# Squares by VectorE's clock, and key weights in a second ring, in a four-layer attention kernel

## The chip, the core and the metric

The kernel runs on one core of a Trainium2 chip. The metric is the device time of one execution in microseconds (us). Instructions run on TensorE (PE in the profile, its weight loads PEld), VectorE (DVE), ScalarE (ACT) and GpSimd (POOL); SyncE's queue (SP) issues all the transfers. Each engine takes its instructions in the order in which they stand in its queue.

## The reference

Four attention layers with a residual each; 2048 tokens, 512 features, 32 heads of 16. Layers 0 and 2 use weights A and a sliding window of 256, layers 1 and 3 weights B and the whole sequence.

```python
def _B_ref(x, wqkv, wo):                  # full; _A_ref adds the window's mask
    B, S, D = x.shape                     # 1, 2048, 512
    H = 32; Dh = D // H
    qkv = (x @ wqkv).reshape(B, S, 3, H, Dh).transpose(2, 0, 3, 1, 4)
    q, k, v = qkv[0], qkv[1], qkv[2]
    p = softmax(einsum("bhqd,bhkd->bhqk", q, k) * Dh ** -0.5)
    o = einsum("bhqk,bhkd->bhqd", p, v)
    return o.transpose(0, 2, 1, 3).reshape(B, S, D) @ wo

x = A_x
x = x + _A_ref(layernorm(x), A_wqkv, A_wo)
x = x + _B_ref(layernorm(x), B_wqkv, B_wo)
x = x + _A_ref(layernorm(x), A_wqkv, A_wo)
x = x + _B_ref(layernorm(x), B_wqkv, B_wo)
```

## The kernel before

**Scores.** A full layer works in quads of four heads (qd, 8 of them; two quads are a head tile) and in four chunks c of 512 queries. For a quad and a chunk, each of 16 key tiles gives two scores s (two heads each, 128 keys x 1024): TensorE multiplies kt by qt (L756), ScalarE takes the exponential of the 128 x 1024 score (e<-s, L764), and TensorE multiplies e by the values into acc (L809). A quad so has 32 scores and a full layer 1024. Layer 1 runs chunk by chunk, layer 3 head tile by head tile (t, four of 256 scores). After a quad, `epilogue` joins the two halves of acc on VectorE (sa, ot), divides (op), and every second quad stores oh, the input of the output projection.

**The softmax's shift.** No maximum of a score is taken. Instead half the sum of the largest squared key and the squared query is subtracted: rows of -0.515 times the squares stand beside q and k, so the score's matmul subtracts them. For that every projection of keys or queries leaves squares sq (GpSimd, L528; ScalarE in the tails, L526). A job `rest` in the list `pend` later sums them over the 16 dims on TensorE (`squares`: a matmul with hsum, L550, in the tails L553), and VectorE makes of the sums the maximum km of the keys (L569) or the queries' row m (L584, L585), which a transfer writes beside the queries in DRAM (qs<-m, L597). `key_shift` makes the keys' row mk out of km (L608, L613) and writes it to kf. The scores' operands qt and kt are read from qs and kf, so these must be there first.

**Side work.** Projections of other chunks, head tiles or layers (L400: 48 matmuls of 512 columns, two halves of the rows each, for 128 features; 96 of 256 columns for values), layer norm and the output projection run between the scores. `Work` is one of them: K1, K3 keys of a head tile for layers 1 and 3; Q3 queries; VV values; OO, O3 output projection; T transposes. `Side` deals them out: after every second score of a quad `step` calls `share`, which first may run the due jobs of `pend` and then one or several matmuls' worth of the projection under way. What it decides by are clocks of a model: `clock[0]` for TensorE, `vt_[0]` for VectorE, `PH["free"]` for the bank. `PH["busy"]` says that a projection is half done. `finish` forces what is left at the end of a stage (a chunk in layer 3). The result is an order written out for TensorE, and in full layers for VectorE too; the other engines' orders come from the tile scheduler.

**The bank.** In a full layer all this side work has one pair of PSUM banks, b (`PH["halves"]`): a projection, or a set of squares, must have been read by VectorE before the next one may begin.

**Weights.** `weights` takes a buffer from one of two rings: ring 0, tag w, two buffers; ring 1, tag vw, three buffers, in the windowed layers used for value tiles. `may_open` says when a load may be issued. Work marked `act` runs in the tail behind a windowed layer, where neither kind of attention runs: `tails[0]` ends with the last chunk's K1(0) and K1(1), `tails[2]` with K3(3, 0), and then the next layer's first values come (`lasts`).

Of the kernel before, what the change touches and what calls it, by code (L numbers as in the profile page):

```python
# [190 lines left out]
def fast_path(ctx, tc, flag, a_x, a_wqkv, a_wo, b_wqkv, b_wo, out):  # L191
# [293 lines left out]
    def project(l, s, c, act, ht=None):  # L485
# [3 lines left out]
        w = weights(ty, s, n, *((0, D, 0) if ht is None else (ht * P, (ht + 1) * P, l == 3 and not act)))  # L489
# [70 lines left out]
    def keys(l, c, act, ht=None, then=None):  # L560
        sqs = yield from project(l, 1, c, act, ht)

        def rest():
            ph = squares(f"k{l}_{c}_{ht}", sqs)
            if l not in KM:
                KM[l] = vp.tile([P, NQ], F32, name=f"km{l}", tag="km", bufs=2)
            r = quarters(ht)
            with tc.high_priority(HEAD_START):
                nc.vector.tensor_reduce(KM[l][r, c:c + 1], ph[r], axis=AX.XY if PH["full"] else AX.X, op=ALU.max)  # L569
                if then is not None:  # L570
                    then(l, ht)
        pend.append((clock[0] + (4.6 if PH["full"] else 3.6), rest))

    def queries(l, c, act, ht=None):
        sqs = yield from project(l, 0, c, act, ht)
# [22 lines left out]
        pend.append((clock[0] + (4.6 if PH["full"] else 3.6), rest))  # L598
# [111 lines left out]
    def epilogue(l, c, qd, a):  # L710
# [14 lines left out]
        def scaled():  # L725
            den = ot[:, :, DH]
            nc.vector.tensor_tensor(lmin, lmin, den, ALU.min)
            nc.vector.tensor_add(lsum, lsum, den)
            r = vp.tile([P, QC // 32], F32, name=f"r{n}", tag="r")
            nc.vector.tensor_scalar_max(r, den, L_MIN)  # L730
            nc.vector.reciprocal(r, r)
            if u == 0:
                OT[t] = vp.tile([P, QC // 32, 2, DH], F32, name=f"op{n}", tag="op", bufs=1)
            nc.vector.tensor_tensor(OT[t][:, :, u, :], ot[:, :, :DH], r[:, :, None].broadcast_to([P, QC // 32, DH]), ALU.mult)

# [114 lines left out]
    class Work:  # L850
# [25 lines left out]
        def may_open(self):  # L876
# [4 lines left out]
                    (len(wused[self.ring]) < RINGS[self.ring] or wused[self.ring][-RINGS[self.ring]].done) and (PH["full"] or not self.ring)  # L881
# [31 lines left out]
    class Side:  # L913
# [65 lines left out]
        def share(self):  # L979
# [3 lines left out]
            if pend and not PH["busy"] and clock[0] >= max(PH["free"], pend[0][0]):  # L983
                settle(False)
                PH["free"] = clock[0] + 2.0
                self.lag += 0.1
# [9 lines left out]
        def finish(self, keep=False):  # L996

            stays = lambda w: (w.name is None and keep) if w.name is None else w.name[0] == "P"
            while any(not stays(w) for w in self.q):
                self.one(True)  # L1000
# [87 lines left out]
    def K3(c, ht, act=False):  # L1088
        return Work(later(keys, 3, c, act, ht, key_shift if c == NQ - 1 and ht == 0 else None), PK / 4, ("K3", c, ht), [("T", 3, c)], True, ring=not act)

    def Q3(c, ht, act=False, after=()):
        return Work(later(queries, 3, c, act, ht), PK / 4, ("Q3", c, ht), [("T", 3, c), *after], True, ring=not act)

    def K1(ht, act=False):
        return Work(later(keys, 1, NQ - 1, act, ht, key_shift), PK / 4, ("K1", ht), [("T", 1, NQ - 1), ("P", 1, 1)], True)

    def shift3(ht):
        def gen():
            settle()
            key_shift(3, ht)  # L1100
            yield -1e-6
        return Work(gen(), 0.0, ("S3", ht), [("K3", c, ht) for c in range(NQ)])
# [115 lines left out]
    def side3(t, c):  # L1218
        a = [last_lower(3)] if (t, c) == (0, 0) else []
        a += [Q3(c + 1, t)] if c < 3 else []  # L1220
        if t < 3:
            a.append(K3(c, t + 1))
            if c == 3:
                a += [shift3(t + 1), Q3(0, t + 1)]
        if t < 2 and (t or c > 1):
            a.append(upper(3, 2 * t + c // 2, range(2 * (c % 2), 2 * (c % 2) + 2)))
        if (t, c) != (0, 0):
# [7 lines left out]
             2: [VV(3, 0, True, (0,)), OO(2, 3, True), VV(3, 1, True, (0,), late(3)), VV(3, 2, True, (0,), late(3)), VV(3, 0, True, (1,), late(3)), T(3, 3), K3(3, 0, True)]}  # L1235
# [54 lines left out]
```

## Time and profile before

| | us |
|---|---|
| timed runs | 2723.14, 2723.62, 2728.02; median 2723.62 |
| profiled execution, its own time | 2721.88 |
| its span | 2720.2 |
| busy: TensorE / ScalarE / VectorE / GpSimd | 2487.6 / 2363.1 / 1110.8 / 526.7 |
| layer 1, first to last exponential | 474.23 to 1425.45 |
| layer 3, first to last exponential | 1746.01 to 2700.19 |
| tail behind layer 0, behind layer 2 | 48.3, 45.1 |

The times below are from the profiled execution; its span is shorter than its time by 1.7 us. The granted TensorE clock over the whole execution was 0.988 of full speed. In a row of a timeline stand the start, the busy time, engine, line and operation, out<-in, the number of instructions, and in brackets the idle time ahead of it and what ended it.

### The profile page before, as it was taken

How to read it: one execution, taken by the hardware profiler on the slowest of the kernel's cores; microseconds unless marked ns; L12 is line 12 of the kernel's file. 1: busy time of each engine (PE TensorE's matmuls, PEld its weight loads, DVE VectorE, ACT ScalarE, POOL GpSimd, SP SyncE). 2: the span in 40 equal slices, each digit the busy share in tenths (PEclk: the TensorE clock that was granted, in tenths of full speed). 3: DMA queues.
4: the chain of work that ended last, by engine and by line, in shares of the span. 5: the costliest groups of instructions: out<-in, count | busy, mean ns of one | idle time of the engine just before them, and what ended most of it. 6: DMA issues, size and time to landing. Idle time of an engine off the chain costs nothing.

```text
span 2720.2 us, 113346 instructions
## 1 busy us (share of the span) xinstructions
PE 2487.6 (91%) x51023; PEld 1095.7 (40%) x51023; DVE 1110.8 (41%) x2342; ACT 2363.1 (87%) x2671; POOL 526.7 (19%) x1080
## 2 busy tenths in 40 slices
PE   7888999999998999999998999899999999988997
PEld 3233444444443444444443333544444444433332
DVE  5574554223434334334326666323333323333333
ACT  4575664999999999999995777499999999999996
POOL 1455551001100100100105778000000000000000
PEclk9999999999999999999999999999999999999999
DMA  8888865222324225333426565623233333334332
GB/s 283 233 253 248 241 193 162 82 90 86 108 91 126 92 90 138 94 100 102 110 71 192 160 194 148 167 72 117 81 107 100 96 96 105 109 106 123 122 118 98
DMA packets 341159, 360.80 MB, mean 133 GB/s; under 512 B 117800, under 2 KB 256568, under 8 KB 334392
## 3 DMA queue, kind: packets, MB, share of 16 engines
q1 hardware_dynamic: 340664, 353.46, 43.7%
q8 instruction: 401, 6.57, 1.0%
q14 instruction: 94, 0.77, 0.1%
HBM read 240.65 MB, written 96.99 MB: 124 GB/s over the span
## 4 chain that ended last, share of the span: by engine, by line
ACT 55%; PE 23%; issue 11%; DVE 7%; DMA 3%; POOL 1%; SPq 0%; ACTq 0%; DVEq 0%; POOLq 0%
ACT e L764 55%; PE b L403 9%; PE acc L842 4%; PE s L760 2%; PE acc L809 2%; PE s L756 2%; PE bs L403 1%; PE b L400 1%; DVE xh L455 1%; DVE xh L449 1%; DMA kt<-kw 1%; DVE xn L449 0%; DVE ot L723 0%; DMA wr<-in_A_wo_dram 0%; DMA wv<-wd 0%
## 5 line engine op out<-in xcount | busy, mean ns | idle before, releaser
L764 ACT ACTIVATE e<-s 128x1024 f32<-128x1024 f32 (+2 forms) x2432 | 2240.7, 1056 | 149.9 <-PE s L760 101.0
L809 PE MATMUL acc<-e,vt 64*17 64x512 f32 x16384 | 1085.6, 590 | 1.0 <-issue 1.0
L756 PE MATMUL s<-qt,kt 64*32 64x512 f16 x16384 | 850.8, 381 | 121.4 <-ACT e L764 99.8
L756 PEld LDWEIGHTS <-kt 64*32 64x32 f16 x16384 | 407.0, 89 | 931.3 <-issue 852.0
L809 PEld LDWEIGHTS acc<-e,vt 64*17 64x17 f32 x16384 | 281.0, 92 | 61.8 <-issue 3.8
L835 POOL TENSOR_SCALAR_AFFINE_SELECT e<-e 128x256 f32<-128x256 f32 x512 | 224.9, 445 | 189.7 <-ACT e L764 188.5
L832 POOL TENSOR_SCALAR_AFFINE_SELECT e<-e 128x256 f32<-128x256 f32 x448 | 199.2, 450 | 94.4 <-ACT e L764 91.9
L842 PE MATMUL acc<-e,vt 128*17 128x384 f32 (+2 forms) x2816 | 201.8, 394 | 6.4 <-POOL e L832 6.2
L741 POOL TENSOR_TENSOR oh<-o,oh 128x512 f16<-128x512 f32 x31 | 36.1, 1163 | 702.0 <-DVE oh L740 676.0
L403 PE MATMUL b<-xc,w 128*128 128x512 f16 x660 | 161.7, 392 | 9.8 <-DVE km L569 5.5
L706 DVE SCALAR_TENSOR_TENSOR x<-b,x 128x512 f32<-128x512 f32 x122 | 83.9, 688 | 193.1 <-PE b L400 189.8
L760 PE MATMUL s<-qt,kt 64*128 64x384 f16 (+2 forms) x1408 | 121.3, 279 | 43.7 <-ACT e L764 20.4
L422 DVE TENSOR_SCALAR sa<-acc 128x512 f32<-128x512 f32 x64 | 44.2, 691 | 281.4 <-PE acc L809 281.4
L528 POOL TENSOR_TENSOR sq_h<-sp_h 128x512 bf16<-128x512 f16 x29 | 42.9, 1479 | 546.4 <-DVE sp_h L522 537.6
L528 POOL TENSOR_TENSOR sq<-sp 128x512 bf16<-128x512 f16 x32 | 46.2, 1443 | 519.7 <-DVE sp L522 475.2
L400 PE MATMUL b<-xc,w 64*32 64x512 f16 x3072 | 126.5, 376 | 2.7 <-DVE j L423 1.5
L400 PE MATMUL b<-xc,w_h 64*32 64x512 f16 x2784 | 111.0, 376 | 3.9 <-DVE km L569 3.9
L400 PE MATMUL b<-wo,oh 64*32 64x512 f16 x2592 | 109.1, 376 | 5.4 <-DVE x L706 3.0
L403 PEld LDWEIGHTS <-w 128*128 128x128 f16 x720 | 67.0, 100 | 116.3 <-issue 46.4
L422 DVE TENSOR_SCALAR vt<-b 128x256 f32<-128x256 f32 (+1 forms) x36 | 18.4, 512 | 232.9 <-PE b L400 232.9
L760 PEld LDWEIGHTS <-kt 64*128 64x128 f16 x1408 | 52.0, 95 | 140.9 <-issue 114.8
L422 DVE TENSOR_SCALAR j_h<-b 128x512 f32<-128x512 f32 x29 | 20.0, 689 | 206.6 <-PE b L400 206.6
(134 smaller groups left out, 1905.9 us busy)
## 6 DMA issues: line engine op xcount, KB each, us to landing
kt<-kf SPq DMA_DIRECT2D x128, 512.0 KB
qt<-qs SPq DMA_DIRECT2D x128, 256.0 KB
xd<-x SPq DMA_DIRECT2D x96, 256.0 KB
x<-xd SPq DMA_DIRECT2D x96, 256.0 KB
w<-wd SPq DMA_DIRECT2D x21, 1024.0 KB
kt<-kw SPq DMA_DIRECT2D x64, 256.0 KB
qs<-sp SPq DMA_DIRECT2D x48, 256.0 KB
wo<-wd SPq DMA_DIRECT2D x12, 1024.0 KB
```

Source lines behind the costliest of these rows:

```text
L400: nc.tensor.matmul(ps[g:g + 32, r], a[k, g:g + 32], b[k], start=(i == 0), stop=(i == len(pairs) - 1), skip_group_check=True)
L403: nc.tensor.matmul(ps, a, b, start=(i == 0), stop=(i == len(pairs) - 1))
L422: nc.vector.tensor_scalar(dst, ps[0], scale, None, op0=ALU.mult)
L528: nc.gpsimd.tensor_tensor(sq, sp[:, 0], sp[:, 0], ALU.mult)
L706: nc.vector.scalar_tensor_tensor(xs[i], p, 1 / WS, xs[i], op0=ALU.mult, op1=ALU.add)
L756: nc.tensor.matmul(ps[g:g + 32, h], kt[R * h:R * h + R, pr, kc + g:kc + g + 32], qt[R * h:R * h + R, pr], start=True, stop=True, skip_grou ...
L760: nc.tensor.matmul(ps[:, h, s0:s0 + wd_], kt[R * h:R * h + R, pr, kc:kc + P], qt[R * h:R * h + R, pr, qc:qc + wd_], start=True, stop=True)
L764: nc.scalar.activation(e[:, :, w0:w1], ps[:, :, w0:w1], AF.Exp, scale=SCALE)
L809: nc.tensor.matmul(acc[r][32 * h:32 * h + DH + 1, :], V[l, qd // 4, j // 8][k, j % 8, 4 * (qd % 4) + h, :], es_[h // 2][k, h % 2, :], star ...
L832: nc.gpsimd.affine_select(v, v, pattern=[[0, 2], [-1, P]], compare_op=ALU.is_gt, fill=0.0, base=0, channel_multiplier=1)
L835: nc.gpsimd.affine_select(v, v, pattern=[[0, 2], [1, P]], compare_op=ALU.is_ge, fill=0.0, base=0, channel_multiplier=-1)
L842: nc.tensor.matmul(a[32 * h:32 * h + DH + 1, q * P:(q + nb) * P], V[l, (4 * c + j) // 4][:, j % 4, 4 * qd + h, :], es_[h // 2][:, h % 2, s ...
```

## The change

It has six parts. (1) In the tails the key weights of K1(0), K1(1) and K3(3, 0) come from ring 1 instead of ring 0; `may_open` allows ring 1 wherever no windowed attention runs. (2) Outside attention a job of `pend` falls due 1.2 us after its projection by the model instead of 3.6. (3) `share` runs such a job only when VectorE's modelled clock, less 0.2, has passed as well. (4) `finish` goes on while a projection is half done and a job is pending. (5) The work `shift3`, which ran all pending jobs and then formed a head tile's shift ahead of Q3(0, t+1), is gone: each head tile's shift is formed in the job of its last keys, K3(3, ht). (6) In `epilogue`, lmin and lsum are updated behind the division.

```diff
@@ -482,11 +482,11 @@
             yield "wait", XNR[l, c] + 2.3 * i
             transposed(l, c, i, xh)
 
-    def project(l, s, c, act, ht=None):
+    def project(l, s, c, act, ht=None, ring=0):
 
 
         ty, n = l % 2, f"{l}_{s}_{c}" + ("" if ht is None else f"_h{ht}")
-        w = weights(ty, s, n, *((0, D, 0) if ht is None else (ht * P, (ht + 1) * P, l == 3 and not act)))
+        w = weights(ty, s, n, *((0, D, 0) if ht is None else (ht * P, (ht + 1) * P, ring)))
         yield wait(8)
         xc = XC[l, c]
         if s == 0:
@@ -557,8 +557,8 @@
 
         return slice(0, P) if ht is None else slice(32 * ht, 32 * ht + 32)
 
-    def keys(l, c, act, ht=None, then=None):
-        sqs = yield from project(l, 1, c, act, ht)
+    def keys(l, c, act, ht=None, then=None, ring=0):
+        sqs = yield from project(l, 1, c, act, ht, ring)
 
         def rest():
             ph = squares(f"k{l}_{c}_{ht}", sqs)
@@ -569,10 +569,10 @@
                 nc.vector.tensor_reduce(KM[l][r, c:c + 1], ph[r], axis=AX.XY if PH["full"] else AX.X, op=ALU.max)
                 if then is not None:
                     then(l, ht)
-        pend.append((clock[0] + (4.6 if PH["full"] else 3.6), rest))
-
-    def queries(l, c, act, ht=None):
-        sqs = yield from project(l, 0, c, act, ht)
+        pend.append((clock[0] + (4.6 if PH["full"] else 3.6 if PH["win"] else 1.2), rest))
+
+    def queries(l, c, act, ht=None, ring=0):
+        sqs = yield from project(l, 0, c, act, ht, ring)
 
         def rest():
             ph = squares(f"q{l}_{c}_{ht}", sqs)
@@ -595,7 +595,7 @@
                     nc.vector.tensor_scalar(m, ph, kx, -0.515, op0=ALU.add, op1=ALU.mult)
             for t in sqs:
                 nc.sync.dma_start(rows(qs[l % 2, c])[8 * t:8 * t + 8, 3, :], m[32 * t:32 * t + 8, :])
-        pend.append((clock[0] + (4.6 if PH["full"] else 3.6), rest))
+        pend.append((clock[0] + (4.6 if PH["full"] else 3.6 if PH["win"] else 1.2), rest))
 
     def settle(all_=True):
         while pend and (all_ or pend[0][0] <= clock[0]):
@@ -724,14 +724,14 @@
 
         def scaled():
             den = ot[:, :, DH]
-            nc.vector.tensor_tensor(lmin, lmin, den, ALU.min)
-            nc.vector.tensor_add(lsum, lsum, den)
             r = vp.tile([P, QC // 32], F32, name=f"r{n}", tag="r")
             nc.vector.tensor_scalar_max(r, den, L_MIN)
             nc.vector.reciprocal(r, r)
             if u == 0:
                 OT[t] = vp.tile([P, QC // 32, 2, DH], F32, name=f"op{n}", tag="op", bufs=1)
             nc.vector.tensor_tensor(OT[t][:, :, u, :], ot[:, :, :DH], r[:, :, None].broadcast_to([P, QC // 32, DH]), ALU.mult)
+            nc.vector.tensor_tensor(lmin, lmin, den, ALU.min)
+            nc.vector.tensor_add(lsum, lsum, den)
 
         def parts():
             o = vp.tile([P, QC], F32, name=f"o{n}", tag="o", bufs=1)
@@ -878,7 +878,7 @@
             return (all(d in DONE for d in self.deps if d[0] == "P") and
                     all(d[1:] in ONR or d[1] % 2 == 0 and d[2] for d in self.deps if d[0] == "O") and
                     all(("N",) + d[1:] in DONE for d in self.deps if d[0] == "T") and
-                    (len(wused[self.ring]) < RINGS[self.ring] or wused[self.ring][-RINGS[self.ring]].done) and (PH["full"] or not self.ring)
+                    (len(wused[self.ring]) < RINGS[self.ring] or wused[self.ring][-RINGS[self.ring]].done) and not (PH["win"] and self.ring)
                     and not (self.adds and any(x.adds and not x.done for x in wused[0])))
 
         done = begun = open = going = False
@@ -980,7 +980,7 @@
 
             self.budget = min(self.budget + max((self.cost - self.spent) / max(self.steps - 3 - self.k, 1), self.least), 0.75)
             self.lag = max(self.lag - 0.42, -0.3)
-            if pend and not PH["busy"] and clock[0] >= max(PH["free"], pend[0][0]):
+            if pend and not PH["busy"] and clock[0] >= max(PH["free"], pend[0][0], vt_[0] - 0.2):
                 settle(False)
                 PH["free"] = clock[0] + 2.0
                 self.lag += 0.1
@@ -996,7 +996,7 @@
         def finish(self, keep=False):
 
             stays = lambda w: (w.name is None and keep) if w.name is None else w.name[0] == "P"
-            while any(not stays(w) for w in self.q):
+            while any(not stays(w) for w in self.q) or PH["busy"] and pend:
                 self.one(True)
             carried.extend(self.q)
 
@@ -1085,21 +1085,15 @@
         k = [("K", l, i) for i in (c - 1, c) if i >= 0] if l % 2 == 0 else list(after)
         return Work(later(queries, l, c, act), PK, ("Q", l, c), [("T", l, c), ("P", l % 2, 0)] + k, True)
 
-    def K3(c, ht, act=False):
-        return Work(later(keys, 3, c, act, ht, key_shift if c == NQ - 1 and ht == 0 else None), PK / 4, ("K3", c, ht), [("T", 3, c)], True, ring=not act)
+    def K3(c, ht, act=False, ring=None):
+        ring = not act if ring is None else ring
+        return Work(later(keys, 3, c, act, ht, key_shift if c == NQ - 1 else None, ring), PK / 4, ("K3", c, ht), [("T", 3, c)], True, ring=ring)
 
     def Q3(c, ht, act=False, after=()):
-        return Work(later(queries, 3, c, act, ht), PK / 4, ("Q3", c, ht), [("T", 3, c), *after], True, ring=not act)
+        return Work(later(queries, 3, c, act, ht, not act), PK / 4, ("Q3", c, ht), [("T", 3, c), *after], True, ring=not act)
 
     def K1(ht, act=False):
-        return Work(later(keys, 1, NQ - 1, act, ht, key_shift), PK / 4, ("K1", ht), [("T", 1, NQ - 1), ("P", 1, 1)], True)
-
-    def shift3(ht):
-        def gen():
-            settle()
-            key_shift(3, ht)
-            yield -1e-6
-        return Work(gen(), 0.0, ("S3", ht), [("K3", c, ht) for c in range(NQ)])
+        return Work(later(keys, 1, NQ - 1, act, ht, key_shift, act), PK / 4, ("K1", ht), [("T", 1, NQ - 1), ("P", 1, 1)], True, ring=act)
 
     def O3(c, ht):
         return Work(wo_part(c, ht), PO / 4, None, [("O", 3, c, ht)], True)
@@ -1221,7 +1215,7 @@
         if t < 3:
             a.append(K3(c, t + 1))
             if c == 3:
-                a += [shift3(t + 1), Q3(0, t + 1)]
+                a.append(Q3(0, t + 1))
         if t < 2 and (t or c > 1):
             a.append(upper(3, 2 * t + c // 2, range(2 * (c % 2), 2 * (c % 2) + 2)))
         if (t, c) != (0, 0):
@@ -1232,7 +1226,7 @@
              [side3(t, c) for t in range(NHT) for c in range(NQ)]]
     late = lambda l: [("N", l, 3)]
     tails = {0: [VV(1, 2, True, (0,)), OO(0, 3, True), VV(1, 1, True, (0, 1), late(1)), VV(1, 0, True, (1,), late(1)), T(1, 3), K1(0, True), K1(1, True)],
-             2: [VV(3, 0, True, (0,)), OO(2, 3, True), VV(3, 1, True, (0,), late(3)), VV(3, 2, True, (0,), late(3)), VV(3, 0, True, (1,), late(3)), T(3, 3), K3(3, 0, True)]}
+             2: [VV(3, 0, True, (0,)), OO(2, 3, True), VV(3, 1, True, (0,), late(3)), VV(3, 2, True, (0,), late(3)), VV(3, 0, True, (1,), late(3)), T(3, 3), K3(3, 0, True, True)]}
     lasts = {l: [VV(l + 1, 3, True, (0,), (), range(2))] for l in (0, 2)}
     for l in range(4):
         if l % 2 == 0:
```

How this moves instructions. First SyncE's queue in tail 0, as a difference (before with -, after with +). w_1_3_h are the weights of K1(0) and K1(1), wv_3_0 those of the values that follow, x the residual's rows, sp_1_3_h the projected keys.

```order
 L477 DMA_TRANSPOSE xc_3_5388<-xh_3_3_5403 128x8x128
 L469 DMA x_3_12044<-xd 128x512
-L371 DMA w_1_3_h_5472<-wd_1_110 128x8x128
-L371 DMA w_1_3_h_5530<-wd_1_110 128x8x128
-L371 DMA wv_3_0_0_5552<-wd_2_111 128x8x256
-L533 DMA kf<-sp_1_3_h_0_5545 128x2x512
-L534 DMA kf<-sp_1_3_h_0_5545 128x512
+L371 DMA wv_3_0_0_5476<-wd_2_111 128x8x256
```

The two key weights leave this place (the first now stands in the last chunk of layer 0, the second ahead of the load of wv_1_0_0 in the early tail), and the value weights follow the last x load. In tail 2 the load of K3(3, 0)'s weights moves in the same way into layer 2, to the place of Q3(1, 0)'s, which goes into the tail.

Next TensorE in layer 3, the squares of the last keys of head tile 2 (sq3_1_3_h2; s3_3_2 and s3_3_3 are scores of the two quads of head tile 1, last chunk). Before:

```order
L756 MATMUL s3_3_2_13_1_44094<-qt3_3_2_43491,kt3_3_2_1_43495 32x512
L550 LDWEIGHTS hsum_86
L550 MATMUL b3_33394<-sq3_1_3_h2_2_44071,hsum_86 32x512
L550 LDWEIGHTS hsum_86
L550 MATMUL b3_33394<-sq3_1_3_h2_2_44071,hsum_86 32x512
L400 LDWEIGHTS w3_0_0_h2_43559
L400 MATMUL b3_33394<-xc3_0_30736,w3_0_0_h2_43559 32x512
```

After:

```order
L756 MATMUL s3_3_3_6_1_44536<-qt3_3_3_43540,kt3_3_3_0_43542 32x512
L550 LDWEIGHTS hsum_86
L550 MATMUL b3_33396<-sq3_1_3_h2_2_44185,hsum_86 32x512
L550 LDWEIGHTS hsum_86
L550 MATMUL b3_33396<-sq3_1_3_h2_2_44185,hsum_86 32x512
L756 LDWEIGHTS kt3_3_3_0_43542
L756 MATMUL s3_3_3_7_0_44555<-qt3_3_3_43540,kt3_3_3_0_43542 32x512
```

The squares stand 18 scores later, and scores follow them where a projection (L400) on the same bank followed before; the next user of b comes four or five scores later.

Last TensorE in layer 3, the squares of Q3(1, 1) (sq3_0_1_h1) and K3(0, 2) (sq3_1_0_h2). Before, the first of them:

```order
L756 MATMUL s3_0_3_4_1_39999<-qt3_0_3_39098,kt3_0_3_0_39100 32x512
L550 LDWEIGHTS hsum_86
L550 MATMUL b3_33394<-sq3_0_1_h1_1_39655,hsum_86 32x512
L550 LDWEIGHTS hsum_86
L550 MATMUL b3_33394<-sq3_0_1_h1_1_39655,hsum_86 32x512
L756 LDWEIGHTS kt3_0_3_0_39100
L756 MATMUL s3_0_3_5_0_40023<-qt3_0_3_39098,kt3_0_3_0_39100 32x512
```

After, both:

```order
L756 MATMUL s3_0_3_8_1_40226<-qt3_0_3_39098,kt3_0_3_1_39102 32x512
L550 LDWEIGHTS hsum_86
L550 MATMUL b3_33396<-sq3_0_1_h1_1_39655,hsum_86 32x512
L550 LDWEIGHTS hsum_86
L550 MATMUL b3_33396<-sq3_0_1_h1_1_39655,hsum_86 32x512
L550 LDWEIGHTS hsum_86
L550 MATMUL b3_33396<-sq3_1_0_h2_2_40013,hsum_86 32x512
L550 LDWEIGHTS hsum_86
L550 MATMUL b3_33396<-sq3_1_0_h2_2_40013,hsum_86 32x512
L756 LDWEIGHTS kt3_0_3_1_39102
L756 MATMUL s3_0_3_9_0_40246<-qt3_0_3_39098,kt3_0_3_1_39102 32x512
```

Before, the keys' squares stood 12 scores behind the queries'; now one set follows the other on b, eight scores later than the first stood. Such pairs stand at five places of layer 3, and at none before. At the program's end the last output projection but one (O3(2, 3), L400) is dealt out over earlier scores, so that none of it is left behind the last score; before, 32 of its matmuls stood there.

## The prediction

> **What bounds the kernel now.** I read the page first, then one table of stages, then the chain of waits and the timelines at the stage ends and at the holes in ScalarE's row. Each row of the table is a stretch, its length, and the busy time of each engine in it:
>
> ```profile
> core 0: us, PE busy (x) PEld busy (x) DVE busy (x) ACT busy (x) POOL busy (x), PEclk, DMA share, GB/s
> 426.00:474.20 48.20, 44.29 (x278) 24.71 (x270) 20.89 (x51) 11.73 (x26) 1.95 (x6) 0.96 0.56 162
> 474.20:1425.50 951.30, 898.88 (x22916) 407.84 (x22924) 337.39 (x666) 944.84 (x1024) 67.73 (x52) 1.00 0.33 98
> 1701.00:1746.00 45.00, 39.37 (x308) 27.18 (x307) 19.19 (x47) 10.59 (x24) 1.12 (x3) 1.00 0.70 192
> 1746.00:2700.20 954.20, 871.78 (x21750) 387.19 (x21742) 309.03 (x580) 943.99 (x1024) 57.23 (x42) 1.00 0.34 104
> 2700.20:2720.20 20.00, 7.18 (x70) 2.27 (x69) 9.84 (x25) 0.00 (x0) 0.00 (x0) 0.79 0.32 110
> ```
>
> The two full layers (rows 2 and 4) hold 70% of the span, and ScalarE's exponentials fill them: 1024 in 951.3 us is 0.93 us a score, and ScalarE is idle for only 6.5 and 10.2 us. So there a change can win no more than those holes, and loses whenever TensorE comes late with a score. In the tails (rows 1 and 3) and at the end TensorE and the chain behind it set the time. The change touches holes, tails and end, so the forecast is a sum of small terms.
>
> **Tail 0: key weights in the other ring.** Before, the first key projection waits for its weights, and the value projection after it for the next ones. Timeline of TensorE, then two pieces of the chain:
>
> ```profile
> 456.63 1.47 PE L403 MATMUL bs<-wv,xc 128*128 128x256 f16 x12
> 457.94 1.47 PE L403 MATMUL b<-wv,xc 128*128 128x256 f16 x12
> 460.49 2.76 PE L403 MATMUL bs<-xc,w_h 128*128 128x512 f16 x12 [1.08 <-DMA w_h<-wd]
> 463.09 2.75 PE L403 MATMUL b<-xc,w_h 128*128 128x512 f16 x12
> 468.41 1.81 PE L403 MATMUL b<-wv,xc 128*128 128x256 f16 x12 [2.24 <-DMA wv<-wd]
> 470.14 0.61 PE L553 MATMUL bs<-sq_h,hsum 128*32 128x512 bf16 x1
> 456.91 3.53 DMA w_h<-wd
> 463.28 5.08 DMA wv<-wd
> ```
>
> Starts of equal groups lie 1.31 us apart (456.63, 457.94) for 256 columns and 2.60 (460.49, 463.09) for 512. With both key weights in place the keys run from 457.94 + 1.31 = 459.25 to 464.45. The value weights now follow the last x load at 456.91, in the place where w_h stood; 3.53 to 5.08 us later is 460.4 to 462.0, before 464.45. One value group of 1.31 and the first squares bring the second squares (L553, which the first scores wait for) to 466.0 instead of 470.14: **-4.1** (-3.4 to -4.4; everything behind L553 moves along). Cover: the new weights must land during layer 0's end and early tail. If they only swap places with the value weights in a busy stretch, one wait of 1.08 to 2.24 comes back. The Trainium skill, "DMA: Bandwidth & Descriptors", Issuing engines are not separate DMA queues, says that all transfers share the same 16 engines and interleave; that speaks against a gain from reordering them alone. By that rule the tails' two terms would be 0 where the engines are full, and the sum -0.4. This tail's row shows a DMA share of 0.56, so that case is a rival below, priced from rows.
>
> A rule on the clock: the Trainium skill, "TensorE: Matmul & The Clock Gate", What's actually happening, has the clock fall to half after an idle window of about 3.4 us. The trace differs, since here
>
> ```profile
> 468.40:471.00 2.60, 2.59 (x15) 1.53 (x16) 0.21 (x1) 0.38 (x1) 0.00 (x0) 0.70 0.86 267
> 477.00:480.00 3.00, 3.00 (x80) 1.25 (x65) 0.00 (x0) 2.02 (x3) 0.00 (x0) 0.56 0.92 284
> ```
>
> ```profile
> 480.05 4.69 ACT L764 ACTIVATE e<-s 128x1024 f32<-128x1024 f32 x5 [0.99 <-PE s L756]
> ```
>
> 0.70 was granted after TensorE had idled 2.24 us, and 0.56 with 0.99 us of hole behind it. A tail with less idle time may start layer 1 without that hole, or only move it: I take 0, bounds -1 to +0.6.
>
> **Tail 2.** The same wait, for one key group:
>
> ```profile
> 1734.66 1.47 PE L403 MATMUL bs<-wv,xc 128*128 128x256 f16 x12
> 1737.46 2.76 PE L403 MATMUL b<-xc,w_h 128*128 128x512 f16 x12 [1.33 <-DMA w_h<-wd]
> ```
>
> Its weights load during layer 2 now, and another load, needed later, takes their old turn: **-1.3** (-0.8 to -1.8).
>
> **Layer 3, the shifts of head tiles 1 to 3.** Before, forming a shift forced the squares out, and the next projection followed on the single bank pair b:
>
> ```profile
> 1938.78 0.41 PE L756 MATMUL s<-qt,kt 64*32 64x512 f16 x8
> 1939.58 0.39 PE L550 MATMUL b<-sq_h,hsum 64*32 64x512 bf16 x2 [0.39 <-POOL sq_h L528]
> 1940.01 1.22 DVE L569 TENSOR_REDUCE km<-b 32x1 f32<-32x1024 f32 x1 [1.38 <-PE b L550]
> 1941.28 0.63 PE L400 MATMUL b<-xc,w_h 64*32 64x512 f16 x16 [1.31 <-DVE km L569]
> 1941.71 0.41 PE L756 MATMUL s<-qt,kt 64*32 64x512 f16 x8
> 1942.25 2.10 ACT L764 ACTIVATE e<-s 128x1024 f32<-128x1024 f32 x2 [1.84 <-PE s L756]
> 2429.13 1.02 ACT L764 ACTIVATE e<-s 128x1024 f32<-128x1024 f32 x1 [1.85 <-PE s L756]
> ```
>
> Score to score took 2.93 us and the hole was 1.84: TensorE's lead is 2.93 - 1.84 = 1.09. There are three such holes (the first and the last are quoted), 5.5 us together. Now these squares run alone, four or five scores ahead of the next user of b, so all go: **-5.5**. The reduction then hides beside the scores; the shift reaches DRAM some 13 us later than before, still 16 scores or more before the keys' first use.
>
> **The price: squares in pairs.** Squares now also wait for VectorE's modelled clock, and so a query job and a key job fall due in one step. In the new order that happens five times, all in layer 3: two sets of squares back to back on b, and the next score behind both. A single set before:
>
> ```profile
> 2209.70 0.41 PE L756 MATMUL s<-qt,kt 64*32 64x512 f16 x8
> 2209.95 0.38 PE L550 MATMUL b<-sq_h,hsum 64*32 64x512 bf16 x2
> 2210.37 0.69 DVE L584 TENSOR_SCALAR m<-b 32x512 f16<-32x512 f32 x1 [2.48 <-PE b L550]
> 2210.47 0.41 PE L756 MATMUL s<-qt,kt 64*32 64x512 f16 x8
> 2211.09 0.69 DVE L585 SCALAR_TENSOR_TENSOR m<-b,m 32x512 f16<-32x512 f32 x1
> 2213.17 0.38 SPq L779 DMA_DIRECT2D qt<-qs  x1
> ```
>
> Alone it costs nothing: score to score 0.77, under the lead. In a pair the second set waits until L585 has read b, 2211.78, which is 2.08 after the score; with its own 0.52 (2209.95 to 2210.47) and 0.03 for the release the next score comes 2.63 after the last. 2.63 - 1.09 = 1.54 us of hole, five times: **+7.7** (6.0 with part of the wait hidden, 9.3 at the shift's 1.85 each).
>
> **Places where an evacuation meets a projection.** Where b is used in the first scores of a quad, VectorE is busy with the last quad's output:
>
> ```profile
> 2673.93 0.45 PE L756 MATMUL s<-qt,kt 64*32 64x512 f16 x8
> 2675.13 0.63 PE L400 MATMUL b<-wo,oh 64*32 64x512 f16 x16 [0.76 <-DVE x L706]
> 2675.56 0.41 PE L756 MATMUL s<-qt,kt 64*32 64x512 f16 x8
> 2676.09 1.02 ACT L764 ACTIVATE e<-s 128x1024 f32<-128x1024 f32 x1 [0.54 <-PE s L756]
> ```
>
> 2675.56 - 2673.93 = 1.63, minus the lead 0.54: the same arithmetic as above. The trace has ten holes of this kind, 0.28 to 0.70, in all 5.1 us; in the new order the pattern (a user of b ending three scores into a quad, the next one at six) stands at five boundaries, 2.7 us: **-2.4** (0 to -3.5, since other patterns may take their place).
>
> **Lumps.** A stage's end now finishes a projection under way when squares are pending. The order has three such lumps inside the layers, of 1.29 us each (48 matmuls of 512 columns or 96 of 256), and 16 more matmuls at the end of layer 1.
>
> ```profile
> 1424.23 2.16 PE b L400 x80
> ```
>
> A matmul is 0.027 us, so 48 are 1.29; a score's 0.21 and the lump make 1.5, hole 0.4: two at +0.4. The third, before head tile 2, meets late query squares, which run four scores ahead of their use: from L550 to the qt load is 3.2 us (above) and the load some 2.3 (the chain has one of 4.52), 5.5 against five scores of 0.93 and the lump: +0.7 (0.3 to 3). The end of layer 1: 16 x 0.027 and an evacuation's rest, +0.7. Together **+2.2** (1 to 4.5).
>
> **The end.**
>
> ```profile
> 2700.73 0.84 PE b L400 x24
> 2701.57 1.83 PE acc L809 x32
> 2703.41 0.69 DVE sa L422
> ```
>
> After the last exponential (2700.2) 24 projection matmuls, which waited for x, and 32 value matmuls run. In the new order that projection is done ahead of the last scores; at most 16 value matmuls, 0.92, follow: 2701.15 instead of 2703.4, **-2.2**, and two small VectorE operations leave the chain, -0.2: **-2.4** (-1.5 to -2.9).
>
> **Edits at nothing.** The shorter due time outside attention leaves TensorE's order in the tails and windowed layers as it was. The two small operations moved behind the division lie on VectorE, 32 to 35% busy in the full layers. In layer 1 one query chunk's squares come 47 scores later, and POOL and VectorE wait for a buffer there: 0 to +0.3.
>
> **Sum.** -4.1 - 1.3 - 5.5 - 2.4 - 2.4 + 7.7 + 2.2 = -5.8. The profiled execution took 2721.88 us (span 2720.2); 2716.1 after. The median of the timed runs is 1.74 above it, so on its scale 2723.62 - 5.8 = 2717.8. About 0.2%, 5.4 us, is what a measurement of this kernel can tell from no change, so faster begins below 2718.2: the forecast lies on that edge.
>
> **Rivals.**
> *The loads only trade places.* Tail 0 keeps a wait of 2.1 and tail 2 its 1.33: 3.4 less gain, 2721.2. For it: the DMA share was 0.86 to 1.03 in stretches of tail 0 and 0.70 over tail 2. Against: no bytes are added, and the new loads start earlier, before those stretches. Chance 0.15. (The Trainium skill's rule on the 16 engines, cited above, is this case.)
> *Pairs and lumps cost their upper bounds* (1.85 a pair, late qt load 3): +1.6 + 2.3, 2721.7. For it: POOL's squares were late by 0.39 at 1939.58. Against: squares that wait longer find POOL done. 0.15.
> *Pairs are nearly hidden*, 0.54 each like the evacuations: -5.0, 2712.8. It takes a lead of 2.1; the three places above all give 1.09. 0.12.
> *Slower: VectorE is behind its modelled clock at the pairs.* If m stands behind a quad's output (three operations, about 0.7 each, 2.1), each pair costs 3.6: +10.5, 4.7 above before, 2728.3. It decides from 1.2 us of delay a pair on. Against: VectorE had idled 2.48 before L584, and the five pairs stand 14 to 18 scores into a quad, far from its output. 0.08.
> *The change doesn't do what it says*: in the new order the two rings and the shifts have moved as described, so this case has no weight beyond the first rival.
>
> **Chances.** The forecast has 0.50; within its own spread of some 3 us I give 0.35 to the faster side of 2718.2 and 0.15 to no difference. With 0.12 for hidden pairs faster is 0.47; the first two rivals and part of the slower one, which lies 4.7 above before, make no difference 0.46; slower by over 0.2% keeps 0.07. The range 2713 to 2723.5 takes in hidden pairs nearly, both rivals below 2722 and the bounds of evacuations and lumps; the slower case is left out.
>
> **What would show it.** Right: TensorE's key groups in tail 0 without a DMA wait and L553 at about 466; in tail 2 a key group right behind the value group; no wait for km in front of L400 in layer 3; five holes near 1.5 us behind pairs of L550, the second waiting for m; at the end no L400 after the last exponential. Wrong: a DMA wait left at the key groups, pairs without a hole or over 2 us, a long hole at the first score of head tile 2, or a layer 1 whose holes differ from 6.5 us by more than 3.

## The result, and the profile after

The changed kernel's median is 2721.64 us in 12 runs (2717.54 to 2725.55), that of the kernel before in 12 runs 2726.39 (2722.83 to 2729.96). The ratio is 0.9983, 95% interval 0.9975 to 0.9991: about 4.7 us, clear of noise and just under the 0.2% that the prediction drew as its line. The profiled execution's span fell from 2720.2 to 2715.7, 4.5 us.

The stages of the changed kernel, in the same table as in the prediction (stretch and length; busy time and number of instructions of PE, PEld, DVE, ACT and POOL; granted clock, share of the DMA engines' time, GB/s):

```profile
426.00:470.05 44.05, 42.40 (x278) 24.25 (x270) 20.80 (x51) 11.74 (x27) 2.27 (x7) 1.00 0.59 170
470.05:1422.70 952.65, 898.96 (x22892) 408.56 (x22900) 337.00 (x666) 944.93 (x1024) 66.99 (x52) 1.00 0.32 98
1422.70:1426.45 3.75, 3.75 (x101) 1.38 (x85) 1.66 (x3) 0.00 (x1) 0.20 (x1) 1.00 0.62 190
1426.45:1698.00 271.55, 249.00 (x2545) 94.53 (x2543) 170.06 (x408) 193.43 (x228) 201.51 (x480) 0.99 0.61 175
1698.00:1741.20 43.20, 39.14 (x300) 27.22 (x298) 19.09 (x47) 10.62 (x24) 1.13 (x3) 1.00 0.72 197
1741.20:2697.80 956.60, 874.63 (x21798) 388.19 (x21798) 310.00 (x582) 944.31 (x1024) 57.24 (x42) 1.00 0.34 104
2697.80:2715.70 17.90, 6.09 (x30) 1.80 (x22) 8.00 (x22) 0.00 (x1) 0.00 (x0) 0.68 0.22 79
```

From first to last exponential, against the kernel before: tail 0 -4.2, layer 1 +1.4, the step to layer 2 +0.8, layer 2 -0.9, tail 2 -1.8, layer 3 +2.4, the end -2.1; sum -4.4. Tails and end gave 8.1 back, and half of it was spent in the full layers again, although three holes of 1.84 us left them.

Tail 0 and tail 2, TensorE's timeline:

```profile
457.87 1.47 PE L403 MATMUL b<-wv,xc 128*128 128x256 f16 x12
459.18 2.75 PE L403 MATMUL bs<-xc,w_h 128*128 128x512 f16 x12
461.77 2.75 PE L403 MATMUL b<-xc,w_h 128*128 128x512 f16 x12
466.19 0.39 PE L553 MATMUL bs<-sq_h,hsum 128*32 128x512 bf16 x1
1731.81 1.47 PE L403 MATMUL bs<-wv,xc 128*128 128x256 f16 x12
1733.12 2.75 PE L403 MATMUL b<-xc,w_h 128*128 128x512 f16 x12
1737.30 0.39 PE L553 MATMUL b<-sq_h,hsum 128*32 128x512 bf16 x1
1740.72 0.41 PE L756 MATMUL s<-qt,kt 64*32 64x512 f16 x8 [1.62 <-DMA kt<-mk]
```

No key group waits for weights now; each starts 1.31 us behind the value group's start, and the second squares of tail 0 stand at 466.19 (forecast 466.0).

A pair of squares in layer 3, the first of five alike:

```profile
1842.77 0.41 PE L756 MATMUL s<-qt,kt 64*32 64x512 f16 x8
1842.98 0.39 PE L550 MATMUL b<-sq_h,hsum 64*32 64x512 bf16 x2
1844.12 0.68 DVE L585 SCALAR_TENSOR_TENSOR m<-b,m 32x512 f16<-32x512 f32 x1
1844.86 0.39 PE L550 MATMUL b<-sq_h,hsum 64*32 64x512 bf16 x2 [1.48 <-DVE m L585]
1844.86 0.60 PE L756 MATMUL s<-qt,kt 64*32 64x512 f16 x8
1845.60 1.02 ACT L764 ACTIVATE e<-s 128x1024 f32<-128x1024 f32 x1 [1.21 <-PE s L756]
```

The second set waits for m, as forecast; the hole is 1.21 us, at 1845, 2027, 2148, 2268 and 2387: 6.05 together.

The late squares of layer 1, which the prediction had put at 0 to 0.3:

```profile
784.16 0.41 PE L550 MATMUL b<-sq,hsum 64*32 64x512 bf16 x8
784.70 4.66 POOL L528 TENSOR_TENSOR sq<-sp 128x512 bf16<-128x512 f16 x4 [8.43 <-PE b L550]
785.78 1.25 DVE L522 CAST sp<-j 128x512 f16<-128x512 f32 x1 [3.38 <-POOL sq L528]
787.06 1.41 DVE L523 TENSOR_TENSOR sp<-j,sp 128x512 f16<-128x512 f32 x1
788.39 0.68 DVE L584 TENSOR_SCALAR m_None<-b 128x512 f16<-128x512 f32 x1
789.85 0.63 PE L400 MATMUL b<-wo,oh 64*32 64x512 f16 x16 [1.82 <-DVE m_None L585]
790.81 2.10 ACT L764 ACTIVATE e<-s 128x1024 f32<-128x1024 f32 x2 [1.52 <-PE s L756]
```

GpSimd could not write the next chunk's squares until these had been read (8.43 us idle). VectorE's conversion waited for GpSimd, and the evacuation m stood behind that conversion in VectorE's order; m began 4.2 us after the squares, and the next projection waited for it.

And the first score of head tile 2, behind the lump of 96 matmuls:

```profile
2220.21 1.51 PE L400 MATMUL b<-wv,xc 64*32 64x256 f16 x96
2222.51 0.41 PE L756 MATMUL s<-qt,kt 64*32 64x512 f16 x8 [0.80 <-DMA qt<-qs]
2223.05 2.10 ACT L764 ACTIVATE e<-s 128x1024 f32<-128x1024 f32 x2 [1.43 <-PE s L756]
```

The queries land 0.80 us after the lump is done. The other lumps cost 0.42 (590) and 0.44 (2101); behind the latter a second hole of 0.45 stands two scores on (2103), and a like pair of holes follows the lump of runs 2 and 5 (0.44 with 0.80 and 0.47).

### The profile page after: what moved, and what is told of

It is laid out like the page before. It is cut to its first block, busy times and chain, and to the rows that moved or that the text cites. A ratio compares the mean times of both kernels' runs of the same rounds, so it can differ in the third digit from the quotient of the medians.

```text
span 2715.7 us, 113355 instructions
## 1 busy us (share of the span) xinstructions
PE 2488.0 (92%) x51023; PEld 1096.7 (40%) x51023; DVE 1100.6 (41%) x2342; ACT 2363.7 (87%) x2671; POOL 528.7 (19%) x1080
## 4 chain that ended last, share of the span: by engine, by line
ACT 56%; PE 23%; issue 11%; DVE 6%; DMA 3%; POOL 1%; SPq 0%; ACTq 0%; DVEq 0%; POOLq 0%
ACT e L764 55%; PE b L403 10%; PE acc L842 4%; PE acc L809 2%; PE s L760 2%; PE bs L403 2%; PE s L756 2%; PE b L400 1%; DVE xh L449 1%; DVE xh L455 1%; DMA kt<-kw 1%; DVE xn L449 1%; DVE ot L723 0%; POOL e L832 0%; DMA wr<-in_A_wo_dram 0%
## 5 line engine op out<-in xcount | busy, mean ns | idle before, releaser
L760 PE MATMUL s<-qt,kt 64*128 64x384 f16 (+2 forms) x1408 | 122.3, 281 | 43.2 <-ACT e L764 19.8
L400 PE MATMUL b<-xc,w 64*32 64x512 f16 x3072 | 126.1, 376 | 1.9 <-DVE x L682 0.8
L400 PE MATMUL b<-wo,oh 64*32 64x512 f16 x2592 | 109.1, 376 | 4.1 <-DVE m_None L585 1.8
L400 PE MATMUL b<-xc,w_h 64*32 64x512 f16 x2784 | 111.8, 376 | 0.0
L422 DVE TENSOR_SCALAR j_h<-b 128x512 f32<-128x512 f32 x29 | 20.1, 692 | 214.8 <-PE b L400 214.8
```

Source lines behind the costliest of these rows:

```text
L400: nc.tensor.matmul(ps[g:g + 32, r], a[k, g:g + 32], b[k], start=(i == 0), stop=(i == len(pairs) - 1), skip_group_check=True)
L422: nc.vector.tensor_scalar(dst, ps[0], scale, None, op0=ALU.mult)
L760: nc.tensor.matmul(ps[:, h, s0:s0 + wd_], kt[R * h:R * h + R, pr, kc:kc + P], qt[R * h:R * h + R, pr, qc:qc + wd_], start=True, stop=True)
```

## The experiments

| run | ratio to before | 95% | layer 1, us | tail 0, us | layer 3, us | end, us |
|---|---|---|---|---|---|---|
| before | | | 951.2 | 48.3 | 954.2 | 20.0 |
| the change | 0.9983 | 0.9975 to 0.9991 | 952.6 | 44.1 | 956.5 | 17.9 |
| 1 rings alone | 0.9983 | 0.9974 to 0.9993 | 952.6 | 43.2 | 955.1 | 20.2 |
| 2 shift alone | 0.9997 | 0.9986 to 1.0009 | 950.2 | 47.2 | 951.2 | 24.3 |
| 3 gate alone | 1.0032 | 1.0022 to 1.0043 | 951.0 | 47.3 | 962.4 | 18.2 |
| 4 change, five sq buffers | 0.9996 | 0.9986 to 1.0005 | 952.4 | 44.1 | 959.4 | 17.4 |
| 5 change, no gate | 0.9982 | 0.9971 to 0.9994 | 952.5 | 44.1 | 949.3 | 22.4 |
| 6 one set at a time | 0.9944 | 0.9924 to 0.9965 | 950.9 | 44.1 | 945.8 | 20.1 |
| 7 sooner bank | 0.9958 | 0.9944 to 0.9973 | 949.4 | 44.1 | 956.8 | 18.1 |
| 8 mixed | 0.9939 | 0.9926 to 0.9953 | 948.5 | 44.1 | 949.8 | 18.0 |
| 9 as 7, two buffers m | 0.9948 | 0.9933 to 0.9964 | 948.3 | 44.1 | 955.2 | 18.1 |

Stages are from the one profiled execution of each. Layer 0 ends between 423.1 and 430.1 us and layer 2 takes 271.6 to 274.8 in them, though the experiments hardly touch these stages: so a difference of some us in one span tells little, and the stages and holes are what is compared. Parts 2, 4 and 6 of the change (due time, `finish`, lmin and lsum) have no run of their own. Scores are counted over both full layers, so layer 3 begins at 1024.

**1. The rings alone**, on the kernel before.

```diff
-    ... and (PH["full"] or not self.ring)
+    ... and not (PH["win"] and self.ring)
-    K1: later(keys, 1, NQ - 1, act, ht, key_shift) ... True)
+    K1: later(keys, 1, NQ - 1, act, ht, key_shift, act) ... True, ring=act)
-    tails[2]: ... K3(3, 0, True)
+    tails[2]: ... K3(3, 0, True, True)
```

> The kernel before with the change of rings alone. Theory (the tails wait for key weights, and the ring removes that): tail 0 falls from 48.3 to 44.1 us and tail 2 from 45.1 to about 43.5; layer 1 gets one lump of 48 matmuls at score 128, a hole of 0.4; the three long holes of layer 3 stay at 1.84. Sum -5.3, about 2721 on the median's scale. Rival (the loads only trade places on the shared transfer engines, the tails gain by the shorter due time): tail 0 stays above 46.5 and tail 2 at 45, sum between 0 and -2.

```profile
427.17:470.36 43.19, 42.44 (x282) 24.25 (x270) 20.84 (x51) 11.74 (x27) 2.41 (x8) 1.00 0.60 174
1699.87:1744.74 44.87, 38.87 (x300) 27.37 (x298) 19.19 (x47) 10.62 (x25) 1.13 (x3) 1.00 0.73 197
1740.74 0.39 PE L553 MATMUL bs<-sq_h,hsum 128*32 128x512 bf16 x1
1744.20 0.41 PE L756 MATMUL s<-qt,kt 64*32 64x512 f16 x8 [3.06 <-DMA kt<-mk]
```

No key group waits for weights in either tail, and tail 0 fell as expected, so the gain there is the rings'. Tail 2 came out at 44.9, not 43.5, nearly the rival's 45. Its squares (1740.74) stand behind both value groups, those of the change (1737.30) ahead of the last one; so mk is late, and the first score waits 3.06 us for it instead of 1.62. Run 1 keeps the due time of 3.6 us, and all runs with the new rings and 1.2 wait 1.61 or 1.62, so in this tail the shorter due time is the likely reason; no run takes it away alone. Over all profiles tail 2 is 42.8 to 44.9 with the new rings and 45.1 to 47.5 without. The three holes of 1.84 stayed, and the lump at score 128 (0.42) came with the rings, not with the stage's end. The rival falls by tail 0 and by the time. Alone, this part is worth as much as the whole change.

**2. The shift alone**, on the kernel before.

```diff
-    key_shift if c == NQ - 1 and ht == 0 else None
+    key_shift if c == NQ - 1 else None
-                a += [shift3(t + 1), Q3(0, t + 1)]
+                a.append(Q3(0, t + 1))
```

> The kernel before with the shift alone moved into the job of the last keys (no separate step that forces the squares). Theory: the three holes of 1.84 us in layer 3 go, one lump of 96 value matmuls stands at score 1472 of the two full layers together (+0.4), and 56 instead of 32 projection matmuls stand behind the last score (+0.7); the tails and the end's wait for x stay. Sum -4.4. Rival (the squares still meet a busy bank, the holes move with them): three holes of 1 us or more at the squares' new places, sum above -2.

The holes of 1.84 are gone from layer 3, which fell by 2.9, and with them the rival. But the time did not fall: the end grew by 4.3, not 0.7. TensorE there, and a stretch of it in the columns of the stage table:

```profile
2700.95 0.84 PE L400 MATMUL b<-wo,oh 64*32 64x512 f16 x24 [1.54 <-DVE x L706]
2703.33 1.48 PE L400 MATMUL b<-wo,oh 64*32 64x512 f16 x24 [1.54 <-DVE x L706]
2704.56 3.66 PE L809 MATMUL acc<-e,vt 64*17 64x512 f32 x32
2702.13:2708.95 6.82, 4.89 (x56) 1.11 (x55) 3.12 (x5) 0.00 (x0) 0.00 (x0) 0.50 0.27 96
```

A group of 24 projection matmuls left behind the last score costs a wait of 1.54 for the one bank besides its own time, and what followed here ran at a granted clock of 0.50: 1.48 instead of 0.84 for 24 matmuls, 3.66 for the 32 value matmuls that took 1.83 before. Run 5 shows the same matmuls without the low clock.

**3. VectorE's clock as a condition alone**, on the kernel before.

```diff
-            if pend and not PH["busy"] and clock[0] >= max(PH["free"], pend[0][0]):
+            if pend and not PH["busy"] and clock[0] >= max(PH["free"], pend[0][0], vt_[0] - 0.2):
```

> The kernel before with VectorE's clock as a condition for the squares alone. Its order has four pairs of squares, the three shift steps as before, and the late squares of a query chunk in layer 1. Theory: four holes of 1.2 us, one of 1.5 in layer 1, the three of 1.84 stay, a lump at score 1472 (+0.4), and nothing of the projection left behind the last score (-2): +4.8 +1.5 +0.4 +0.2 -2 = +4.9, slower. Rival (the gate itself is harmless and takes away the small holes at quad starts): small holes fall from 5.1 to 2.7 and the pairs are hidden, -4.

```profile
796.58 1.02 ACT L764 ACTIVATE e<-s 128x1024 f32<-128x1024 f32 x1 [1.52 <-PE s L756]
2042.29 1.02 ACT L764 ACTIVATE e<-s 128x1024 f32<-128x1024 f32 x1 [1.21 <-PE s L756]
```

Slower, by 0.32% (some 8.7 us, more than the expected 4.9). Four holes of 1.21 and the one of 1.52 stand where expected and the shift's three remain; layer 3 took 8.2 more. The gate did not take away small holes at the quad starts either: seven of 0.54 or 0.55 stand in layer 3. The rival falls. The step to layer 2 grew to 3.8 and the end fell to 18.2, both as in the change, so these two are the gate's.

**4. One more buffer for the squares**, on the changed kernel.

```diff
-                sq = vp.tile([P, QC], BF16, name=f"sq{n}_{t}", tag="sq", bufs=NHT)
+                sq = vp.tile([P, QC], BF16, name=f"sq{n}_{t}", tag="sq", bufs=NHT + 1)
```

> The changed kernel with five buffers instead of four for the squares' inputs in the tag sq. Theory for the hole of 1.52 us in layer 1 (GpSimd waits for a buffer of squares, VectorE's conversion stands behind GpSimd, and the squares' own evacuation stands behind that conversion): with a fifth buffer the conversion is done earlier, the evacuation follows the squares at once, and the hole goes; all else stays as in the changed kernel: -1.5 against it. Rival (the squares' place in the order alone makes the hole): it stays at 1.5.

```profile
784.49 0.41 PE L550 MATMUL b<-sq,hsum 64*32 64x512 bf16 x8
785.03 3.04 POOL L528 TENSOR_TENSOR sq<-sp 128x512 bf16<-128x512 f16 x3 [8.42 <-PE b L550]
785.05 0.69 DVE L584 TENSOR_SCALAR m_None<-b 128x512 f16<-128x512 f32 x1 [1.08 <-PE b L550]
788.16 0.63 PE L400 MATMUL b<-wo,oh 64*32 64x512 f16 x16
1838.04 1.02 ACT L764 ACTIVATE e<-s 128x1024 f32<-128x1024 f32 x1 [0.18 <-ACT e L764]
```

m follows the squares at once and the projection waits for nothing: the hole of 1.52 is gone, so its cause is the chain of buffers. The time did not fall with it: 0.9996 to before, an interval that overlaps that of the change. Layer 1 is only 0.2 shorter, since two holes stand in it that the change has not (0.74 at 512.94, 0.58 at 1387.58). Layer 3 took 959.4 instead of 956.5, and the exponentials' starts show where: once in every 64 scores one begins 1.14 to 1.21 us after the one ahead, where the change has 0.90 or 0.91 at the same scores. The sixteen together make 4.0 us, and two small holes less (0.44 and 0.52) take 1.0 off. The last line above is one of the sixteen: its row names no other engine, and its score had been done since 1837.66. The last section comes back to such gaps.

**5. The change without the gate.**

```diff
-            ... max(PH["free"], pend[0][0], vt_[0] - 0.2):
+            ... max(PH["free"], pend[0][0]):
```

> The changed kernel without VectorE's clock as a condition for the squares (part 3 undone). Its order has no pairs, the squares of layer 1 at their old place, one lump at score 1472 instead of those at 1408 and 1536, and 56 projection matmuls behind the last score instead of none. Theory (the gate makes pairs that cost 1.21 us each and the hole of 1.52; but it also clears the end): layer 3 about 951 us instead of 956.5, layer 1 about 951, the end 24.3 us as in the run of the shift alone instead of 17.9: -5.5 -1.5 -0.7 +6.4 = -1.3 against the changed kernel. Rival (the end was only slow in that one run, its worth is the 24 matmuls' 0.7): end 20.5, -5 against it.

```profile
2701.20 1.91 PE L809 MATMUL acc<-e,vt 64*17 64x512 f32 x32
```

Layer 3 fell by 7.2 and the end rose by 4.5, and the ratio stayed at 0.998. The gate pays with pairs for an end without projections; neither order of squares is a gain in itself. So far the theory holds. But the end, 22.4, lies midway between its 24.3 and the rival's 20.5: the two groups of 24 wait 1.53 and 1.54 for the bank as in run 2, while the clock was 1.00 and the 32 value matmuls took 1.91 instead of 3.66. So the rest of run 2's end was its clock. Layer 1 lost the hole of 1.52 but not its length (952.5, not 951): holes at quad starts make 2.5 us instead of 1.6, and one of 0.41 came at 517.

**6. One set of squares at a time**, the gate in layer 3 alone (`PH["l"]` is the layer).

```diff
-            ... max(PH["free"], pend[0][0], vt_[0] - 0.2):
-                settle(False)
+            ... max(PH["free"], pend[0][0], vt_[0] - 0.2 if PH["l"] == 3 else 0.0):
+                pend.pop(0)[1]()
```

> The changed kernel with one set of squares at a time, and VectorE's clock as a condition in layer 3 alone. Its order has no pairs, no lump in layer 3, layer 1 without the late squares, and 32 projection matmuls behind the last score, as before the change. Theory (a pair's price is the second set's wait for the first set's evacuation): no hole of 1.21 in layer 3, which falls to about 949.5 to 951; layer 1 about 951; the end 20 us: -6 -1.5 -0.7 +2.1 = -6.1 against the changed kernel, 2715.5. Rival (the squares' cost is in the gate's delay, whether paired or not): five holes near 1 us stay, layer 3 above 954.

```profile
1743.72:2689.48 945.76, 870.22 (x21750) 387.57 (x21751) 306.52 (x580) 942.73 (x1024) 57.52 (x42) 1.00 0.34 104
1844.93 0.39 PE L550 MATMUL b<-sq_h,hsum 64*32 64x512 bf16 x2
1845.47 0.41 PE L756 MATMUL s<-qt,kt 64*32 64x512 f16 x8 [0.15 <-ACT e L764]
1848.61 0.38 PE L550 MATMUL b<-sq_h,hsum 64*32 64x512 bf16 x2
```

The two sets of the first pair now stand 3.7 us apart, and no hole follows either. Layer 3 is 10.8 us shorter than in the change, more than expected: with the pairs went the lumps and the late queries of head tile 2. So the pairing, not the gate's delay, made the price, and the rival falls.

**7. The same with the bank free sooner**, in both layers (1.6 us after the squares by the model instead of 2.0; no lumps, and nothing left at the end).

```diff
-                PH["free"] = clock[0] + 2.0
+                PH["free"] = clock[0] + 1.6
```

> As one set at a time, and the bank counts as free 1.6 us after the squares by the model instead of 2.0, so that the next projection may follow one turn (two scores) after them. Its order has no pairs, no lump at the end of layer 1 or at score 128, and no projection matmul behind the last score. Theory (the squares' evacuation, done 2.1 us after the score ahead of them, fits in two scores of 0.93 and the lead of 1.09): layer 1 about 950.5, layer 3 950 to 951.5, the end 17.9: -10 against the changed kernel, about 2712 and a ratio near 0.9945 to before; the best of all. Rival (two scores are too few, each projection behind a set of squares waits): many holes of 0.5 us in both layers, no better than one set at a time.

Layer 1 and the end came as expected, layer 3 did not (956.8):

```profile
1962.76 0.68 DVE L584 TENSOR_SCALAR m<-b 32x512 f16<-32x512 f32 x1 [2.31 <-DMA kf<-mk]
1964.21 0.63 PE L400 MATMUL b<-wv,xc 64*32 64x256 f16 x32 [2.12 <-DVE m L585]
1965.19 1.02 ACT L764 ACTIVATE e<-s 128x1024 f32<-128x1024 f32 x1 [1.88 <-PE s L756]
```

A query set now follows the last keys' set so soon that m waits for the transfer that still reads mk: both use one buffer. With that wait go holes of 1.88, 1.00 and 1.55. Sixteen gaps of 0.26 in ScalarE's row (last section) make another 4.2, and five holes of 0.54 stand at quad starts, where run 6 has three; so the rival is right in part.

**8. Mixed**: one set at a time, sooner in layer 1, as in run 6 in layer 3, and the last projections dealt out sooner.

```diff
-        yield wait(4)
+        yield wait(3 if t == NHT - 1 and c else 4)
...
+                PH["free"] = clock[0] + (2.0 if PH["l"] == 3 else 1.6)
```

> One set of squares at a time, in layer 1 with the bank free 1.6 us after them and without VectorE's clock, in layer 3 with 2.0 and with it; and the last head tile's output projections are modelled to wait 3 us for their weights instead of 4, so that 8 instead of 32 of their matmuls stand behind the last score. Theory (each part brings what its stage showed): layer 1 about 949.5 and the step to layer 2 1.7 to 2 us, as in the run with the sooner bank; layer 3 about 946 as with one set; the end about 18.5. Against one set at a time -1.5 -1.2 -1.6 = -4.3: about 2707 to 2709, ratio near 0.993 to before. Rival (the end depends on x and the weights that land from DRAM, not on the matmuls' place): the end stays at 20 and a hole or two of 1 us appear in the last 40 scores, where TensorE waits for weights.

The lowest time: median 2707.14, ratio 0.9939. Layer 1 and the end brought what was expected, the step to layer 2 took 1.7 us. Layer 3 was 949.8 instead of 946: ScalarE has 16 gaps of 0.26 us in it that run 6 has not (below). Runs 6 and 8 can't be told apart by their intervals; both beat the kernel before and the change.

**9. Run 7 with two buffers for m and mk** (the same edit at both).

```diff
-  tag="m", bufs=1)
+  tag="m", bufs=2)
```

> The kernel with the sooner bank, and two buffers instead of one for the rows m and mk. In the run with the sooner bank two places of layer 3 have holes of 1.88 + 1.00 and 1.55 us: a head tile's shift mk is still being written to DRAM from the one buffer when the next queries' m is due, VectorE waits 2.0 to 2.3 us for that transfer, and the next projection waits for VectorE. Theory: with a second buffer these holes go, layer 3 falls by about 4 to 4.5. Rival (the projection comes too soon in any case): they stay above 1.

m no longer waits for the transfer, but holes of 1.46 and 1.18 stand near the old places, of another kind:

```profile
1964.69 0.59 PE L809 MATMUL acc<-e,vt 64*17 64x512 f32 x1 [1.08 <-issue]
1965.59 1.02 ACT L764 ACTIVATE e<-s 128x1024 f32<-128x1024 f32 x1 [1.46 <-PE s L756]
```

At both TensorE idled for nothing that the trace shows (1.08 at 1964.69, 1.14 at 2212.84). Layer 3 fell by 1.6 only, so theory and rival are both half right, and the cause of these holes stays open.

## Why the prediction was right, and where it was not

The forecast was 5.8 us of gain on the median's scale, the measurement 4.7. The absolute time, 2721.64, lies above the forecast 2717.8 and in the range, since more runs moved the median of the kernel before from 2723.62 to 2726.39.

- *Tail 0*, -4.1: measured -4.2. The other profiles without the new rings show 47.2 and 47.3 instead of 48.3, so part of it was that execution's. The clock's hole at the start of layer 1 stayed (1.05 at 475.79), as the value 0 took it.
- *Tail 2*, -1.3: measured -1.8; the keys' start is as forecast, and 0.4 is a quicker transfer of mk (1.69 instead of 2.10). The shorter due time stood at nothing, since TensorE's order in the tails is as before; but with the rings alone that order is another (run 1), so here it probably holds up some 1.4 of the gain.
- *The shift*, -5.5: all three holes are gone, here and in run 2.
- *Pairs*, +7.7: 6.05. The mechanism and the count were right, the term was mis-sized. The step that failed is the second set's own 0.52 us. In the pair the next score's first matmuls start with the second set (1844.86), and the score ends 0.60 later. A score takes 0.41 elsewhere, so it came 2.28 after the last one (1844.86 + 0.60 - 0.41 - 1842.77) instead of 2.63; less the lead of 1.09 that is 1.19, and the hole is 1.21. So 0.3 of the 0.52 was slack of a lone set. Half of it is seen in run 6, where the score behind a set waits 0.15 for ScalarE; the other half is not explained. (The lead is read at two places in the prediction's lines, not three.)
- *Evacuations at quad starts*, -2.4: holes of 0.54 stand at just the five boundaries named by the order (2.7), as forecast.
- *Lumps*, +2.2: 0.42 + 0.44 + 1.43 + 0.76 = 3.05. The late queries before head tile 2 were undersized (1.43 with their lump, not 0.7). The cause given, that a stage's end finishes a projection when squares are pending, is not borne out: the lump at 128 is the rings' (run 1); runs 2 and 3, which lack that condition, have one at 1472 (0.44); and run 6, which has it, has none in layer 3. What makes those at 1408 and 1536 no run isolates.
- *Late squares in layer 1*, 0 to +0.3: 1.52. Here the mechanism itself was wrong. It was priced as a wait of GpSimd and VectorE beside the scores; that the evacuation m stands behind the waiting conversion in VectorE's queue was left out.
- *The end*, -2.4: -2.1.

With the measured sizes the terms make -4.2 - 1.8 - 5.5 - 2.4 - 2.1 + 6.05 + 3.05 + 1.5 = -5.4; the span fell by 4.5. Layer 2, for which there is no term, took another 0.9 off, and small holes that no term names gave 1.8 back, 1.4 of them in layer 3 (0.44 at 1749.58, 0.45 at 2103.45, 0.52 at 2424.59). So the sum came out so near partly by luck: pairs 1.6 too dear stood against lumps, late squares and small holes that were too cheap or not there. Of the rivals, swapped loads fell with run 1; nearly hidden pairs, upper bounds (1.85 a pair, queries 3 us late) and VectorE far behind fell with the holes of 1.21 and 1.43.

## What to carry to other kernels

Where one buffer serves two jobs, the second one's price is the first one's evacuation less the lead of the engine that is fed; that lead can be read where the trace has a hole (score to score less hole) and here priced the other place to within a third (1.54 against 1.21). A rule that delays jobs makes them fall due together, so release one at a time. And work taken out of a full stage must be followed to the program's end: what is left there is paid in full, with its waits, and in one of two runs at half the clock. And before a stage's length is put down to an edit, its gaps should be counted: in four of the nine experiments some 4 us of layer 3 are gaps that the edit doesn't explain.

## What the runs showed of the hardware

VectorE's conversion sp took 0.43 us, and the difference behind it 0.69, in run 4, and 1.25 and 1.41 in the change, where GpSimd was squaring at the time (784.70 to 789.36). The Trainium skill, "SBUF — State Buffer", Who interferes with whom, says that VectorE and GpSimd contend for one shared pair of ports, by an exclusive lock. The two longer durations agree with contention; whether it is a lock they do not show. The evacuation from PSUM beside it kept its 0.68.

The granted clock was 1.00 or 0.50 and changed in steps of 3.41 us. In the kernel before it fell 14 times, and in the 3.41 us ahead of a fall TensorE had been busy for 0 to 54%; so it need not idle all that time. One such fall, in tail 0 (stretch, PE's busy time first, clock third from the end):

```profile
466.01:469.42 3.41, 1.17 (x11) 0.92 (x11) 1.34 (x3) 1.09 (x2) 0.00 (x0) 1.00 1.00 302
469.42:472.83 3.41, 3.41 (x17) 1.88 (x15) 1.51 (x4) 0.38 (x1) 0.00 (x0) 0.50 0.47 155
```

Three kernels (7, 8, 9) have a gap of 0.26 us in ScalarE's row once in every 64 exponentials of layer 3, sixteen of them or 4.2 us. Its row names only ScalarE's own work, and the score had been done before. Run 4 has a like delay at another place of the 64; the other profiles have none. That it depends on where the instructions lie is a guess that no run here tests.

```profile
2670.62 1.02 ACT L764 ACTIVATE e<-s 128x1024 f32<-128x1024 f32 x1 [0.26 <-ACT e L764]
```
